# Attention and two MoE layers in one kernel: the sums of s over the later positions taken by one scan for both heads, and later in the lead-in

## Chip, cores and metric

The kernel runs on one core of one Trainium2 chip. The metric is the device time of one execution in microseconds (us); the number quoted for a kernel is the median of its runs.

## What is computed

Three layers follow one another. Attention, for 4 batches and 8 heads of 576 positions and 64 columns, has a bias from running sums of s:

```python
s_pos = np.maximum(s, 0.0)
cum = np.cumsum(s_pos, axis=-1)
bias = -(cum[:, :, :, None] - cum[:, :, None, :])
scores = np.where(causal, -1000000000.0, scores + np.minimum(bias, 0.0))
```

Then softmax over the keys and a product with v. The 2304 x 512 result goes through a first layer, `max(max(x @ w1, x @ w2), x @ w3) @ w_out` with 768 hidden columns, and a second, `((x @ w_a) * (x @ w_b)) @ w_out` with 1536. The change concerns `cum` alone.

## The kernel before

Two heads make a pair; a batch has four pairs, all four 16. A pair is done in two parts: R = 0 is its first 256 positions (`Q0`), R = 1 the other 320 (`N1`). The order of parts is batch by batch, R = 0 of its four pairs, then R = 1. The first layer's products (the gates, `g`, L803) follow each part's output X, with w1, w2, w3 split into a high and a low half (`hg`, `lg`), three products for each block of 128 rows: high by high, low of X by high, high by low. Gate weights come as 18 loads of 512 KB (`wraw`, L244), named w0 to w17 in their order here. Each is made into numbers by ACT (L255) and DVE (L258, L259), rounded by POOL into `hg` (L88), and subtracted by DVE into `lg` (L92). w0, w1, w2 and all from w5 on share three raw buffers, which `lg` frees.

**The lead-in** (`lead_in`, L1051) does R = 0 of the first batch, four pairs p = 0 to 3, before anything else. At the start DVE runs a scan over s of the first 256 positions of both heads (L179): row r of `cum`, on partition 64 + r, holds head 0 in columns 0 to 255 and head 1 in columns 256 to 511, and `reset` puts the sum back to zero between them. The result, multiplied by columns of the identity, becomes extra rows of k and q, so that scores and bias come out of one product. Then for each pair and head: score products on PE (`fs`, L1096), maxima on DVE (L598, one instruction of 128 and one of 256 columns, each with a read of its accumulator), exp and sums on ACT (L605), sum and reciprocal on DVE (L614, L615), the division on POOL (L619, two instructions a head), transposes on PE (`ts`, L710) with copies to SBUF by ACT or DVE (L713), products with v (`pv`, L737), and the split of X into `Xh` (ACT, L81) and `Xl` (DVE, L92). The probabilities have four buffers (tag P), so that pair 2 writes where pair 0 stood, and pair 3 where pair 1 stood.

The sums of the later 320 positions are needed first by R = 1 of this batch. `scan_tails` (L184) makes them after the second pair's maxima: one max with zero over 16 rows x 640 columns (L185), then a scan for each head over 16 x 320 (L188), that begins from the head's sum at position 255, in the same 16 partitions. `store_sums` (L194) writes all sums to DRAM (`ck` for keys, `cq` for queries) by five DMAs on SP's queue; `load_pair` (L494) reads a row of each back into the k and q tiles of a pair, and the first product of R = 1, `fj` (L671), reads those tiles. `store_tails` (L202) later splits the sums in a high and a low half (L204, L205) and stores these (`kt`, `qt`).

What order the instructions of an engine have is settled by a scheduler when the kernel is built, out of priorities (`tc.high_priority`) and its own estimate of each instruction; `issue_after` and, for PE, `on_pe` (L1044) add order by hand. A small edit can therefore change the order for a long way behind it.

Of the kernel before, what the change touches and what calls it, by code (L numbers as in the profile page):

```python
# [29 lines left out]
def kernel(  # L30
# [44 lines left out]
    def f(ap):  # L75
        return ap.bitcast(F32)
# [67 lines left out]
    def pt_tile(shape, dt, nm):  # L144
        return ap_.tile(shape, dt, tag="PT", bufs=2, name=nm)

    def parts(t):

        return (
            t[:, : 2 * Q0].rearrange("r (h c) -> r h c", h=2),  # L150
            t[:, 2 * Q0 : 2 * S].rearrange("r (h c) -> r h c", h=2),
        )

    def spin(n):

        ps = ps_m.tile([P, 512], F32, tag="m", name="spin")
# [11 lines left out]

    cum, sraw = early("KB1"), early("KB2")
    reset, ones = early("QA1")[:, : 2 * Q0], early("QA2")[:, : 2 * Q0]  # L170
    up, rr = slice(64, P), slice(64, 64 + SR)
    with tc.high_priority(5100):
        for a, e in enumerate((nc.sync, nc.scalar, nc.sync, nc.scalar)):
            e.dma_start(sraw[64 + a * SR : 64 + (a + 1) * SR, : 2 * Q0], s[:, : 2 * Q0])
        nc.vector.memset(reset[up], 1.0)
        nc.vector.memset(reset[up, Q0 : Q0 + 1], 0.0)
        nc.vector.memset(ones[up], 1.0)
        nc.vector.tensor_scalar_max(sraw[up, : 2 * Q0], sraw[up, : 2 * Q0], 0.0)
        nc.vector.tensor_tensor_scan(  # L179
            cum[up, : 2 * Q0], reset[up], sraw[up, : 2 * Q0], 0.0,  # L180
            op0=ALU.mult, op1=ALU.add,
        )

    def scan_tails():  # L184
        nc.vector.tensor_scalar_max(sraw[rr, 2 * Q0 :], sraw[rr, 2 * Q0 :], 0.0)  # L185
        for h in range(2):
            c = slice(2 * Q0 + h * N1, 2 * Q0 + (h + 1) * N1)
            nc.vector.tensor_tensor_scan(  # L188
                cum[rr, c], ones[rr, :N1], sraw[rr, c],
                cum[rr, (h + 1) * Q0 - 1 : (h + 1) * Q0],  # L190
                op0=ALU.mult, op1=ALU.add,
            )

    def store_sums(dk, dq, t):  # L194
        a, b = parts(t[rr])
        nc.sync.dma_start(dk[:, :, :Q0], a)
        nc.sync.dma_start(dk[:, :, Q0:], b)
        nc.sync.dma_start(dq[:, 0], b[:, 0])
        nc.sync.dma_start(dq[:, 1, 0:64], b[:, 1, 256:])
        nc.sync.dma_start(dq[:, 1, 64:], b[:, 1, :256])  # L200

    def store_tails():  # L202
        hi = early("KB2", F32R)
        nc.scalar.copy(hi[rr], cum[rr])  # L204
        nc.vector.tensor_tensor(cum[rr], cum[rr], f(hi[rr]), op=ALU.subtract)  # L205
        store_sums(kt[:, 0], qt[:, 0], f(hi))
        store_sums(kt[:, 1], qt[:, 1], cum)

# [367 lines left out]
    def small(nm, w=1):  # L576
        return ap_.tile([P, w], F32, tag="small", bufs=10, name=nm)
# [473 lines left out]
    def lead_in():  # L1051
# [21 lines left out]
                    qq[p][lo_], cum[lo_, : 2 * Q0], AF.Copy, scale=-float(D) ** 0.5  # L1073
                )
        with tc.high_priority(4800):
            nc.sync.dma_start(sraw[rr, 2 * Q0 :], s[0:SR, 2 * Q0 :])
            for p in LP:
                nc.sync.dma_start(lead[p][2], qv0[0, p][:, 2 * Q0 :])
            for j in range(NL):
                fetch_w1(w1_keys[j])  # L1080
# [7 lines left out]
        def fs(p):  # L1088
            for h in range(2):
                pool, tag = (ps_m, "m") if h else (ps_s, "s")  # L1090
                ps = pool.tile([P, 512], F32, tag=tag, name="f0")
                pt = ap_.tile([P, S], F32, tag="P", bufs=4, name="F0")
                for i in range(2):
                    o = ps[:, P * i : P * (2 * i + 1)]
                    def mm(o=o, i=i):
                        last_pe[:] = [nc.tensor.matmul(  # L1096
                            o, two(qq[p])[:, h, i * P : i * P + P],
                            two(kk[p])[:, h, 0 : P * (i + 1)], start=True, stop=True,
                        ).ins]
                    on_pe(mm)  # L1100
                pend.append(sm_a([[(ps[:, 0:P], 0)], [(ps[:, P : 3 * P], P)]], pt, SCALE))
                if len(pend) > 1:
                    with tc.issue_after(pend[-1][-1]):
                        sm_b(pend.pop(0))
                pts[p, h] = pt

        def ts(p):
            if p % 2 == 0:
                shared["PT"] = pt_tile([P, 2, 4 * N1], F32, "PF")
            PF[p] = shared["PT"][:, :, p % 2 * 2 * N1 :]  # L1110
            for h in range(2):
                def tr(h=h):
                    f_t0(PF[p], h, pts[p, h], True)
                on_pe(tr)
# [16 lines left out]

        with tc.high_priority(4000):
            fs(0)
            fs(1)
            with tc.issue_after(pend[-1][-1]):
                scan_tails()
            store_sums(ck, cq, cum)
            fs(2)
            ts(0)
            fs(3)  # L1140
            sm_b(pend.pop(0))
            ts(1)
            pv(0)
            fetch(NP)
            ts(2)
            pv(1)
            fetch(NP + 1)
            ts(3)
            wn()
            pv(2)  # L1150
            wn()
            sp(1)
            pv(3)
            wn(NL - 2)
# [731 lines left out]
```

## Time and profile before

| what | us |
|---|---|
| median of 3 runs (lowest to highest) | 885.6 (884.72 to 887.51) |
| the profiled execution | 884.49 |
| its span, first to last instruction | 882.4 |
| PE busy with matmuls | 869.9 (99%) |
| DVE busy | 632.6 (72%) |
| ACT busy | 394.3 (45%) |
| POOL busy | 210.0 (24%) |

The profile is one execution; 2.1 us of its own time lie outside of the span. Times in the rows further down are us from the start of the span. Engines are PE (matmul; PEld is its weight load), DVE, ACT, POOL, and SP, which issues most DMAs ("SPq"). A matmul's busy time holds its latency, so that neighbours overlap, and two products of one row each cost what their starts are apart. The share of busy time is an average over the span; the lead-in and the stretch behind it differ from it.

### The profile page before, as it was taken

How to read it: one execution, taken by the hardware profiler on the slowest of the kernel's cores; microseconds unless marked ns; L12 is line 12 of the kernel's file. 1: busy time of each engine (PE TensorE's matmuls, PEld its weight loads, DVE VectorE, ACT ScalarE, POOL GpSimd, SP SyncE). 2: the span in 40 equal slices, each digit the busy share in tenths (PEclk: the TensorE clock that was granted, in tenths of full speed). 3: DMA queues.
4: the chain of work that ended last, by engine and by line, in shares of the span. 5: the costliest groups of instructions: out<-in, count | busy, mean ns of one | idle time of the engine just before them, and what ended most of it. 6: DMA issues, size and time to landing. Idle time of an engine off the chain costs nothing.

```text
span 882.4 us, 16782 instructions
## 1 busy us (share of the span) xinstructions
PE 869.9 (99%) x6024; PEld 828.8 (94%) x6024; DVE 632.6 (72%) x1437; ACT 394.3 (45%) x859; POOL 210.0 (24%) x327
## 2 busy tenths in 40 slices
PE   8999999999999999999999999999999999999998
PEld 6767899899999999999999999999999999999998
DVE  7986646575778566664797866777776859987874
ACT  7564745575656545544563323222222224433321
POOL 5445322233423323200003111111111310322211
PEclk9999999999999999999999999999999999999999
DMA  7665634265234853483302134444442353353231
GB/s 231 190 202 175 173 108 130 88 179 149 65 97 116 269 158 122 136 288 122 140 1 72 37 120 137 162 141 159 141 158 93 111 182 123 99 174 129 96 120 49
DMA packets 68219, 120.04 MB, mean 136 GB/s; under 512 B 6920, under 2 KB 50600, under 8 KB 68136
## 3 DMA queue, kind: packets, MB, share of 16 engines
q1 hardware_dynamic: 60944, 111.58, 39.5%
q10 hardware_dynamic: 7192, 7.38, 2.5%
q8 instruction: 48, 0.79, 0.4%
q14 instruction: 35, 0.29, 0.1%
HBM read 87.92 MB, written 31.01 MB: 135 GB/s over the span
## 4 chain that ended last, share of the span: by engine, by line
PE 93%; DVE 3%; DMA 1%; ACT 1%; issue 1%; POOL 1%; ACTq 0%; POOLq 0%; DVEq 0%; SPq 0%
PE X L1252 29%; PE g L803 24%; PE Z L1252 15%; PE Y L1252 8%; PE fpv L737 5%; PE t L755 3%; PE s L627 2%; PE s L628 2%; PE f L671 1%; PE ft L710 1%; DMA wraw<-in_moe_w_dram 1%; PE W L1252 1%; PE tj L768 1%; PE sj L662 1%; PE sj L661 1%
## 5 line engine op out<-in xcount | busy, mean ns | idle before, releaser
L803 PE MATMUL g<-Xh,hg 128*128 128x320 f32 (+1 forms) x576 | 175.1, 307 | 0.6 <-POOL hg L88 0.5
L803 PE MATMUL g<-Xh,lg 128*128 128x256 f32 (+1 forms) x576 | 173.5, 302 | 1.2 <-DVE lg L92 1.2
L803 PE MATMUL g<-Xl,hg 128*128 128x256 f32 (+1 forms) x576 | 172.3, 300 | 0.0
L803 PEld LDWEIGHTS g<-Xh,hg 128*128 128x128 f32 x576 | 108.4, 189 | 5.9 <-issue 2.5
L803 PEld LDWEIGHTS g<-Xh,lg 128*128 128x128 f32 x576 | 108.7, 189 | 3.7 <-DVE lg L92 2.7
L803 PEld LDWEIGHTS g<-Xl,hg 128*128 128x128 f32 x576 | 108.8, 189 | 1.8 <-issue 0.7
L88 POOL TENSOR_SCALAR wh<-wval 128x256 fp32r<-128x256 f32 x77 | 40.9, 540 | 275.5 <-DVE wval L343 226.5
L1252 PE MATMUL X<-xh,wh 128*128 128x384 f32 x288 | 97.2, 338 | 0.0
L1252 PE MATMUL X<-xl,wh 128*128 128x384 f32 x288 | 96.9, 336 | 0.0
L1252 PE MATMUL X<-xh,wl 128*128 128x384 f32 x288 | 96.9, 337 | 0.0
L1252 PE MATMUL X<-woh,slot 128*128 128x256 f32 x408 | 76.6, 281 | 0.5 <-ACT ob L1299 0.5
L619 POOL TENSOR_SCALAR P<-P,rs 128x128 f32<-128x128 f32 (+2 forms) x80 | 48.1, 607 | 101.5 <-DVE rs L615 71.7
L356 DVE TENSOR_TENSOR slot<-hraw,slot 128x768 fp32r<-128x768 f32 x60 | 60.3, 1031 | 13.8 <-POOL slot L88 11.1
L356 DVE TENSOR_TENSOR u<-Z,u 128x384 f32<-128x384 f32 x72 | 39.6, 551 | 37.9 <-ACT u L1299 28.2
L1252 PEld LDWEIGHTS X<-woh,slot 128*128 128x128 f32 x408 | 64.3, 189 | 0.7 <-ACT ob L1299 0.7
L812 DVE TENSOR_TENSOR hf<-g,hf 128x256 f32<-128x256 f32 (+1 forms) x96 | 43.5, 453 | 27.6 <-PE g L803 19.5
L605 ACT ACTIVATE P<-P,nm 128x128 f32<-128x128 f32 (+2 forms) x80 | 46.7, 584 | 35.8 <-DVE nm L598 24.6
L1252 PE MATMUL X<-wol,slot 128*128 128x256 f32 x204 | 57.0, 280 | 0.0
L81 ACT ACTIVATE slot<-hraw 128x768 fp32r<-128x768 f32 x39 | 32.5, 846 | 51.3 <-DVE hraw L356 24.3
L1252 PEld LDWEIGHTS X<-xh,wh 128*128 128x128 f32 x288 | 54.1, 188 | 0.5 <-DVE u L356 0.3
L1252 PEld LDWEIGHTS X<-xl,wh 128*128 128x128 f32 x288 | 54.1, 188 | 0.0
L1252 PEld LDWEIGHTS X<-xh,wl 128*128 128x128 f32 x288 | 54.1, 188 | 0.0
(211 smaller groups left out, 2210.2 us busy)
## 6 DMA issues: line engine op xcount, KB each, us to landing
hT<-u SPq DMA_DIRECT2D x72, 192.0 KB
hraw<-hT SPq DMA_DIRECT2D x36, 384.0 KB
wraw<-in_moe_w_dram SPq DMA_DIRECT2D x18, 512.0 KB
wraw<-in_moe_w_out_dram SPq DMA_DIRECT2D x18, 512.0 KB
kraw<-in_kT_dram SPq DMA_DIRECT2D x24, 288.0 KB
wraw<-in_moe_w_a_dram SPq DMA_DIRECT2D x12, 512.0 KB
wraw<-in_moe_w_b_dram SPq DMA_DIRECT2D x12, 512.0 KB
st<-h1T SPq DMA_DIRECT2D x24, 192.0 KB
```

The source lines that it names most:

```text
L81: return nc.scalar.activation(o, i, AF.Copy, scale=scale)
L88: nc.gpsimd.tensor_scalar(o, i, scale, 1.0, op0=ALU.mult, op1=ALU.mult)
L356: return {"V": nc.vector, "P": nc.gpsimd}[e].tensor_tensor(o, a, b, op=op)
L605: e_ = nc.scalar.activation(pt[:, c0:c1], pt[:, c0:c1], AF.Exp, bias=first, scale=-1.0, accum_out=sm[:, g : g + 1],)
L619: n_ = nc.gpsimd.tensor_scalar(pt[:, c0:c1], pt[:, c0:c1], rs[:, g : g + 1], 1.0, op0=ALU.mult, op1=ALU.mult,)
L627: nc.tensor.matmul(ps, QA1[:, qs], KB1[:, h, ksl], start=True, stop=False)
L628: nc.tensor.matmul(ps, QA2[:, qs], KB2[:, h, ksl], start=False, stop=True)
L737: e_ = nc.tensor.matmul(ps[h * D : h * D + D, c0:n], w, x, start=(t == 0), stop=(t == len(mm[h]) - 1),)
L755: nc.tensor.transpose(ps[:, j * P : j * P + P], pt[:, j * P : j * P + P], ident)
L803: nc.tensor.matmul(ps[:, :n], w[:, kk, :], x[:, kk, :], start=(i == 0), stop=(i == len(mm) - 1),)
L812: st["V"] = nc.vector.tensor_tensor(hf, ps[:, :n], hf, op=ALU.max)
L1252: e_ = nc.tensor.matmul(ps[:, :n], w, x, start=(first and i == 0), stop=(i == len(mm) - 1), skip_group_check=not first,)
```

## The change

The sums of the later positions move to partitions 0 to 63: head 0 of the 16 rows on partitions 0 to 15, head 1 on 32 to 47, both in columns 0 to 319, so that one scan of 64 partitions does both heads. Its initial values, the sums at position 255, lie on other partitions (64 + r): two products on PE with rows of the identity bring them into a PSUM tile (`find_off`), and ACT copies them to SBUF. The rows that no load fills are set to zero by a memset, `ones` is filled on all partitions, and the load of the later s becomes two DMAs. `scan_tails` and `store_sums` are called after the maxima of the last pair instead of the second. Stores of 320 columns that were one DMA for both heads are now two, six DMAs in place of five; `store_tails` makes its split in two pieces (16 x 512 and 64 x 320).

```diff
--- before.py
+++ after.py
@@ -144,13 +144,6 @@
     def pt_tile(shape, dt, nm):
         return ap_.tile(shape, dt, tag="PT", bufs=2, name=nm)
 
-    def parts(t):
-
-        return (
-            t[:, : 2 * Q0].rearrange("r (h c) -> r h c", h=2),
-            t[:, 2 * Q0 : 2 * S].rearrange("r (h c) -> r h c", h=2),
-        )
-
     def spin(n):
 
         ps = ps_m.tile([P, 512], F32, tag="m", name="spin")
@@ -168,41 +161,64 @@
 
     cum, sraw = early("KB1"), early("KB2")
     reset, ones = early("QA1")[:, : 2 * Q0], early("QA2")[:, : 2 * Q0]
-    up, rr = slice(64, P), slice(64, 64 + SR)
+    up, rr, tl = slice(64, P), slice(64, 64 + SR), slice(0, 64)
+    w0 = slice(0, 2 * Q0)
     with tc.high_priority(5100):
         for a, e in enumerate((nc.sync, nc.scalar, nc.sync, nc.scalar)):
-            e.dma_start(sraw[64 + a * SR : 64 + (a + 1) * SR, : 2 * Q0], s[:, : 2 * Q0])
+            e.dma_start(sraw[64 + a * SR : 64 + (a + 1) * SR, w0], s[:, w0])
         nc.vector.memset(reset[up], 1.0)
         nc.vector.memset(reset[up, Q0 : Q0 + 1], 0.0)
-        nc.vector.memset(ones[up], 1.0)
-        nc.vector.tensor_scalar_max(sraw[up, : 2 * Q0], sraw[up, : 2 * Q0], 0.0)
+        nc.vector.memset(ones, 1.0)
+        nc.vector.memset(sraw[tl, :N1], 0.0)
+        nc.vector.tensor_scalar_max(sraw[up, w0], sraw[up, w0], 0.0)
         nc.vector.tensor_tensor_scan(
-            cum[up, : 2 * Q0], reset[up], sraw[up, : 2 * Q0], 0.0,
-            op0=ALU.mult, op1=ALU.add,
+            cum[up, w0], reset[up], sraw[up, w0], 0.0, op0=ALU.mult, op1=ALU.add
         )
 
+    def load_tails():
+        for h in range(2):
+            nc.sync.dma_start(
+                sraw[32 * h : 32 * h + SR, :N1],
+                s[:, 2 * Q0 + h * N1 : 2 * Q0 + (h + 1) * N1],
+            )
+
+    off = []
+
+    def find_off():
+
+        off.append(ps_m.tile([P, 512], F32, tag="m", name="off"))
+        for h in range(2):
+            last_pe[:] = [nc.tensor.matmul(
+                off[0][32 * h : 32 * h + 32, :1], ident[up, 64:96],
+                cum[up, (h + 1) * Q0 - 1 : (h + 1) * Q0], start=True, stop=True,
+            ).ins]
+        o = small("off")
+        nc.scalar.copy(o[tl], off[0][tl, :1])
+        off[0] = o
+
     def scan_tails():
-        nc.vector.tensor_scalar_max(sraw[rr, 2 * Q0 :], sraw[rr, 2 * Q0 :], 0.0)
-        for h in range(2):
-            c = slice(2 * Q0 + h * N1, 2 * Q0 + (h + 1) * N1)
-            nc.vector.tensor_tensor_scan(
-                cum[rr, c], ones[rr, :N1], sraw[rr, c],
-                cum[rr, (h + 1) * Q0 - 1 : (h + 1) * Q0],
-                op0=ALU.mult, op1=ALU.add,
-            )
+        t = sraw[tl, :N1]
+        nc.vector.tensor_scalar_max(t, t, 0.0)
+        nc.vector.tensor_tensor_scan(
+            cum[tl, :N1], ones[tl, :N1], t, off[0][tl], op0=ALU.mult, op1=ALU.add
+        )
 
     def store_sums(dk, dq, t):
-        a, b = parts(t[rr])
-        nc.sync.dma_start(dk[:, :, :Q0], a)
-        nc.sync.dma_start(dk[:, :, Q0:], b)
-        nc.sync.dma_start(dq[:, 0], b[:, 0])
-        nc.sync.dma_start(dq[:, 1, 0:64], b[:, 1, 256:])
-        nc.sync.dma_start(dq[:, 1, 64:], b[:, 1, :256])
+        b = [t[32 * h : 32 * h + SR, :N1] for h in range(2)]
+        nc.sync.dma_start(
+            dk[:, :, :Q0], t[rr, w0].rearrange("r (h c) -> r h c", h=2)
+        )
+        nc.sync.dma_start(dk[:, 0, Q0:], b[0])
+        nc.sync.dma_start(dk[:, 1, Q0:], b[1])
+        nc.sync.dma_start(dq[:, 0], b[0])
+        nc.sync.dma_start(dq[:, 1, 0:64], b[1][:, 256:])
+        nc.sync.dma_start(dq[:, 1, 64:], b[1][:, :256])
 
     def store_tails():
         hi = early("KB2", F32R)
-        nc.scalar.copy(hi[rr], cum[rr])
-        nc.vector.tensor_tensor(cum[rr], cum[rr], f(hi[rr]), op=ALU.subtract)
+        for r, c in ((rr, w0), (tl, slice(0, N1))):
+            nc.scalar.copy(hi[r, c], cum[r, c])
+            nc.vector.tensor_tensor(cum[r, c], cum[r, c], f(hi[r, c]), op=ALU.subtract)
         store_sums(kt[:, 0], qt[:, 0], f(hi))
         store_sums(kt[:, 1], qt[:, 1], cum)
 
@@ -1073,7 +1089,7 @@
                     qq[p][lo_], cum[lo_, : 2 * Q0], AF.Copy, scale=-float(D) ** 0.5
                 )
         with tc.high_priority(4800):
-            nc.sync.dma_start(sraw[rr, 2 * Q0 :], s[0:SR, 2 * Q0 :])
+            load_tails()
             for p in LP:
                 nc.sync.dma_start(lead[p][2], qv0[0, p][:, 2 * Q0 :])
             for j in range(NL):
@@ -1131,13 +1147,14 @@
 
         with tc.high_priority(4000):
             fs(0)
+            on_pe(find_off)
             fs(1)
+            fs(2)
+            ts(0)
+            fs(3)
             with tc.issue_after(pend[-1][-1]):
                 scan_tails()
             store_sums(ck, cq, cum)
-            fs(2)
-            ts(0)
-            fs(3)
             sm_b(pend.pop(0))
             ts(1)
             pv(0)
```

The scheduler orders the program anew: PE's order differs from its first products up to about its 890th row, then it is the same as before. Lines of the changed kernel are 16 or 17 higher from L200 on (its L614 is the maxima, L598 before; its L630 and L631 are sum and reciprocal, its L819 the gates, L687 `fj`). Numbers in names are the scheduler's and differ between the two.

On DVE, in the lead-in, before, from the end of the second pair's maxima (`F_261`) to the third's second head (`F_301`); `eKB` is `cum` or the raw s, `ft` are transposes:

```order
L598 ISA F_261,nm<-f_260,maskJ 128x256
L598 ISA nm 128x1
L185 TENSOR_SCALAR eKB_116<-eKB_116 16x640
L614 TENSOR_SCALAR rs<-sm 128x2
L598 ISA F_285,nm<-f_284,maskJ 128x128
L598 ISA nm 128x1
L188 SCALAR_TENSOR_TENSOR eKB_115<-eQA_118,eKB_115,eKB_116 16x320
L615 RECIPROCAL rs<-rs 128x2
L188 SCALAR_TENSOR_TENSOR eKB_115<-eQA_118,eKB_115,eKB_116 16x320
L598 ISA F_285,nm<-f_284,maskJ 128x256
```

and in the changed kernel, from the last pair's maxima (`F_343`, second head) on:

```order
L729 COPY PF<-ft_375 128x384
L614 ISA F_343,nm<-f_342,maskJ 128x256
L614 ISA nm 128x1
L201 TENSOR_SCALAR eKB_116<-eKB_116 64x320
L630 TENSOR_SCALAR rs<-sm 128x2
L202 SCALAR_TENSOR_TENSOR eKB_115<-eQA_118,off,eKB_116 64x320
L631 RECIPROCAL rs<-rs 128x2
L92 TENSOR_TENSOR Xl<-fpv,Xh 128x256
L729 COPY PF<-ft_404 128x384
L630 TENSOR_SCALAR rs<-sm 128x2
L631 RECIPROCAL rs<-rs 128x2
```

The max and the scan now stand behind the last maxima, ahead of the last pair's two reciprocals (L631).

On PE, at the end of the lead-in, before, from the last product with v:

```order
L737 MATMUL fpv<-PF,kqv 64x256 x2
L737 MATMUL fpv<-PF,kqv 64x128 x2
L671 MATMUL fj<-kraw,qvraw 64x288 x4
L803 MATMUL g<-Xh,hg_0_140 128x256
L803 MATMUL g<-Xl,hg_0_140 128x256
L803 MATMUL g<-Xh,lg_0_141 128x256
```

and in the changed kernel, from the end of the first gate (12 products, here its last two) on:

```order
L819 MATMUL g<-Xl,hg_0_141 128x256
L819 MATMUL g<-Xh,lg_0_142 128x256
L687 MATMUL fj<-kraw,qvraw 64x288 x4
L819 MATMUL g<-Xh,hg_0_143 128x256
L819 MATMUL g<-Xl,hg_0_143 128x256
L819 MATMUL g<-Xh,hg_0_145 128x256
L819 MATMUL g<-Xl,hg_0_145 128x256
L819 MATMUL g<-Xh,hg_1_147 128x256
L819 MATMUL g<-Xl,hg_1_147 128x256
L687 MATMUL f_500<-kraw,qvraw 128x384
```

`fj`, the first product of R = 1, stood ahead of all gates and stands now behind the first gate; behind it come the first two products of each of the next three gates, ahead of the next scores (`f_500`).

On DVE again, some 20 us later, before: the low half of w7 (`lg_2_155`) and of w8 (`lg_2_157`), and the first step of w9 (L258):

```order
L615 RECIPROCAL rs<-rs 128x1
L258 TENSOR_SCALAR wraw<-wraw 128x512
L92 TENSOR_TENSOR lg_2_155<-wraw,hg_2_154 128x512
L598 ISA FJ,nm<-fj,maskJ,nm 128x288
L598 ISA nm 128x1
L92 TENSOR_TENSOR lg_2_157<-wraw,hg_2_156 128x512
```

and in the changed kernel (`lg_2_156` is w7's, `lg_2_158` w8's, L274 the step on w9):

```order
L631 RECIPROCAL rs<-rs 128x1
L92 TENSOR_TENSOR lg_2_156<-wraw,hg_2_155 128x512
L614 ISA FJ,nm<-fj,maskJ,nm 128x288
L614 ISA nm 128x1
L274 TENSOR_SCALAR wraw<-wraw 128x512
L92 TENSOR_TENSOR lg_2_158<-wraw,hg_2_157 128x512
```

w9's first step stood ahead of w7's low half and stands now behind it, still ahead of w8's.

On SP, the first `kt` and `qt` stores of `store_tails` stand now ahead of the loads of the third pair's R = 1 rows, where they stood behind them.

## Rows read from the trace of the kernel before

**Rows 1.** Page, part 1: busy time, share of the span, instructions.
```profile
PE 869.9 (99%) x6024; PEld 828.8 (94%) x6024; DVE 632.6 (72%) x1437; ACT 394.3 (45%) x859; POOL 210.0 (24%) x327
```
**Rows 2.** Waits of PE, 24 to 70 us, the longest: for whom, total, times, longest.
```profile
PE g L803 <- DVE lg L92: 1.2, 2, 0.9
PE t L755 <- POOL F L619: 0.5, 1, 0.5
PE g L803 <- POOL hg L88: 0.5, 1, 0.5
```
**Rows 3.** Waits of PE, 70 us to the end; longest row.
```profile
PE s L628 <- POOL P L619: 1.3, 1, 1.3
```
**Rows 4.** Timeline, the later sums on DVE: start, duration, engine, line, what.
```profile
10.78 0.52 DVE L185 TENSOR_SCALAR eKB<-eKB 16x640 f32<-16x640 f32 x1
...
11.89 0.88 DVE L188 TENSOR_TENSOR_SCAN eKB<-eQA,eKB,eKB 16x320 f32<-16x320 f32 x1
...
12.99 0.87 DVE L188 TENSOR_TENSOR_SCAN eKB<-eQA,eKB,eKB 16x320 f32<-16x320 f32 x1
```
**Rows 5.** Timeline, lead-in: other engines and the last pair's maxima.
```profile
11.51 0.19 ACT L605 ACTIVATION_READ_ACCUMULATOR F<-F,nm 128x1 f32 x1
...
11.97 1.48 PE L1096 MATMUL f<-kqv 128*128 128x128 f32 x8
...
14.64 0.55 DVE L713 COPY PF<-ft 128x384 f32<-128x384 f32 x1
...
17.99 0.41 DVE L598 CUSTOM_DVE_ANT_0 F<-f,maskJ 128x256 f32<-128x256 f32 x1
...
20.12 0.82 POOL L619 TENSOR_SCALAR F<-F,rs 128x128 f32<-128x128 f32 x2 [0.42 <-DVE rs L615]
```
**Rows 6.** Timeline, DVE at the start and at the split of the sums.
```profile
3.41 0.56 DVE L178 TENSOR_SCALAR eKB<-eKB 64x512 f32<-64x512 f32 x1 [0.49 <-DMA eKB<-in_s_dram]
...
55.52 1.73 DVE L205 TENSOR_TENSOR eKB<-eKB,eKB 16x1152 f32<-16x1152 f32 x1
```
**Rows 7.** Timeline, PE from the lead-in's end: `fj`, first gate, first later scores.
```profile
23.84 1.17 PE L671 MATMUL fj<-kraw,qvraw 66*64 66x288 f32 x8
...
24.94 0.39 PE L803 MATMUL g<-Xh,hg 128*128 128x256 f32 x1
...
27.09 0.91 PE L671 MATMUL f<-kraw,qvraw 66*128 66x384 f32 x2 [0.21 <-DVE nm L598]
```
**Rows 8.** Chain that ended last: twelve gate products in a row.
```profile
76.84 1.43 PE g L803 x12
```
**Rows 9.** Timeline, steps of a gate weight, apart and beside each other.
```profile
21.91 0.69 DVE L259 SCALAR_TENSOR_TENSOR wraw<-wraw 128x512 int32<-128x512 int32 x1
...
22.69 0.64 POOL L88 TENSOR_SCALAR hg<-wraw 128x512 fp32r<-128x512 f32 x1 [1.74 <-DVE wraw L259]
...
28.16 1.73 DVE L259 SCALAR_TENSOR_TENSOR wraw<-wraw 128x512 int32<-128x512 int32 x2
...
29.37 2.09 POOL L88 TENSOR_SCALAR hg<-wraw 128x512 fp32r<-128x512 f32 x2 [0.63 <-DVE wraw L259]
```
**Rows 10.** Timeline, SP: stores of the later sums, reads of their rows.
```profile
13.90 0.60 SPq L197 DMA_DIRECT2D ck<-eKB  x1
...
19.14 0.27 SPq L492 DMA_DIRECT2D kraw<-ck  x1
...
20.08 0.22 SPq L492 DMA_DIRECT2D qvraw<-cq  x1
```
**Rows 11.** Timeline, DVE at 45 us: w9's first step, w7's low half.
```profile
45.03 0.43 DVE L258 TENSOR_SCALAR wraw<-wraw 128x512 int32<-128x512 int32 x1 [1.62 <-DMA wraw<-in_moe_w_dram]
...
45.38 0.68 DVE L92 TENSOR_TENSOR lg<-wraw,hg 128x512 fp32r<-128x512 f32 x1
```
**Rows 12.** Busy by stretch: PE, PEld, DVE, ACT, POOL, then granted clock, DMA share, GB/s.
```profile
13.90:17.35 3.45, 2.14 (x14) 1.16 (x14) 2.81 (x18) 2.73 (x11) 2.50 (x7) 1.00 1.04 374
17.35:20.76 3.41, 3.41 (x19) 2.04 (x16) 2.42 (x11) 1.88 (x7) 2.01 (x6) 0.50 0.29 74
```

## The prediction

> **What bounds the kernel now.** I read the busy times first, then the waits of PE, then the timeline of the lead-in. PE is busy for 99% of the span [rows 1]. Its waits from 24 to 70 us are 2.2 us in the three longest rows [rows 2], and of those behind 70 us the longest sum is 1.3 us [rows 3], so from the first gates on PE's own work is nearly the bound, and a change that adds no more to PE than two tiny products can win only what PE loses before that: the lead-in, up to the first gate product at 24.94 [rows 7], and those 2.2 us. All of it together is a small part of 884 us. What lies in the lead-in: DVE does the later sums for 0.52 + 0.88 + 0.87 = 2.27 us between 10.78 and 13.86 [rows 4], with two maxima of the third pair on either side of them. The last pair's last maxima end at 17.99 + 0.41 = 18.40, the last division on POOL at 20.12 + 0.82 = 20.94 [rows 5], and 4.0 us later the gates begin.
>
> **The lead-in, step by step.** Taken out of DVE: 2.27 us ahead of the last maxima [rows 4]. Not all of it comes off, since two other things wait. The last pair's maxima write the buffers from which the second pair is transposed, and those transposes stand on PE behind the last score products, which end at 11.97 + 1.48 = 13.45 [rows 5], unmoved; with three transposes behind them, 0.5, the first of the last maxima can start at 14.0. From there DVE's queue to the last maxima is two heads of 128 and 256 columns (0.41 for the larger, some 0.3 for the smaller), a copy of 0.55 [rows 5], and five sums and reciprocals that run into one another, 1.9 us in all: it ends at 15.9, 2.5 us sooner.
> Put in behind it: a max over 320 columns, between nothing and the 0.52 that 640 columns took [rows 4], taken as 0.35 from 0.56 for 512 [rows 6]; and one scan over 64 x 320. No row has that shape; 16 x 320 took 0.88, and twice that bounds it above. I take 0.88, since the time of DVE's rows goes with columns. The scan ends at 17.2 and the two reciprocals of the last pair come behind it. Between them stand a split of X over 256 columns (0.4, as the maxima of that width) and a copy of 0.55 [rows 5]; with 0.5 for the small ones and POOL's start the last division begins at 18.65 and ends, 0.82 later, at 19.45: 1.5 us sooner than 20.94.
> From the last division to the gates before: 4.0 us, in which `fj` takes 24.94 - 23.84 = 1.1 [rows 7]. `fj` now follows the first gate, so 2.9 remain: gates from 22.35, twelve products in 1.43 [rows 8], done at 23.8. Before, `fj` and that gate were done near 26.4.
>
> **The small edits together.** A zero memset of 320 columns on DVE is shorter than the 0.49 us for which DVE waited for s [rows 6]: nothing, and were that cover gone 0.3. ACT's copy of 64 x 1 stands in the first exps; its nearest row is 0.19 [rows 5], and it moves the second pair's sums by 0.2, which the 14.0 above already hides; between nothing and 0.2. The two products of one column on PE stand where PE waits for maxima anyway; 0 to 0.3 (two of twelve in [rows 8]). One more load of s on SP stands ahead of the gate weights, whose second step runs first at 21.91 [rows 9]: nothing, up to 0.6, one issue as in [rows 10]. The split of the sums on DVE takes 832 columns for 1152: 1.73 x 832 / 1152 = 1.25 [rows 6], 0.5 less, there where PE waited 0.5 for a division [rows 2]; I count 0.2. The `kt` and `qt` stores now block SP in front of the third pair's rows until the split is made; this costs nothing, as the `fj` of that pair stands 28 products further back in PE's new order, some 3 us by [rows 8].
>
> **Behind the lead-in the gain is mostly spent.** After the first gate PE wants weights. The last product with v ends where the gates begin, at 22.35; 0.85 later, for `Xh` and `Xl`, at 23.2, DVE has the last split of X behind it, then three steps L258 (0.43 each, [rows 11]) to 24.4, then four L259 in a row while POOL rounds. Alone a step takes 0.69 and a rounding 0.64; beside each other two took 1.73 and two 2.09 [rows 9], so 0.87 and 1.05. First L259 to 25.1, roundings to 26.0, 27.05 and 28.1. PE's order has products of all three weights ahead of the next scores: these start at 28.1 + 0.24 = 28.35, with 18 gate products done. Before, they started at 27.09 with 14 done [rows 7]. Four products are 0.48, so at this place the new kernel is 1.26 - 0.48 = 0.8 **behind**. The low halves are then all made early, and before the change PE still had waits ahead of it: 0.3 of the 1.2 and the 0.5 of [rows 2], and latency with them, 1.0. Balance at 32 us: 0.2 ahead, and 1.2 if the steps run at their lone times. I take 0.4, near the first, as the four now overlap as those rows did.
> Here a page speaks against the change. The Trainium skill, SBUF — State Buffer, section "Who interferes with whom", says that a DVE instruction with two SBUF inputs and a GpSimd instruction that reads SBUF exclude each other for the whole instruction. Its result is a rival below.
> At 45 us DVE waited 1.62 for w9 and w7's low half stood behind that [rows 11]; PE lost 0.9 there [rows 2]. Now w7's half is ahead of it. w8's is still behind, but PE needs it some 20 products (2.4 us) later, so the 0.9 goes, unless w9 is later: I count 0.7.
>
> **Sum**, against the profiled execution's 884.49: 0.4 + 0.7 + 0.2 = 1.3 sooner, 883.2. The median shown is 885.6, 1.1 above that execution, so the median forecast is **884.3**. A measurement of this kernel can tell about 0.3%, 2.7 us, from no change.
>
> **`fj` and its rows.** The scan ends at 17.2, and five stores follow on SP, at 0.6 each, as the issue of 13.90 took [rows 10]: the last at 19.8. Before, the key row was asked for 19.14 - 13.90 = 5.24 after its store was issued, and `fj` ran 23.84 - 20.08 = 3.76 after the last row was asked for [rows 10, 7]. Both are upper bounds, 28.8 together; below, only the issues count, 20.4. `fj` may start as late as 28.1 - 1.17 - 0.5 = 26.4 without moving anything. I take it as in time: before, the store lay behind weights at a DMA share of 1.04, and the share from 17.35 on was 0.29 [rows 12].
> The Trainium skill, DMA: Bandwidth & Descriptors, section "Anatomy of one DMA — SWDGE (gpsimd) path", gives a fixed cost of some 2 us for a transfer on another kind of queue; by it, an estimate, `fj` would start near 24.1, and the sum would stay. No run here shows a transfer alone.
>
> **Rivals.**
> *The lead is kept whole*: conversions at lone times and no wait in their place. 2.6 of the lead-in and 0.9 at 45 us, 3.5 in all: 882.1. For it: POOL stood idle for 1.74 ahead of its first rounding [rows 9]. Against it: the four steps in a row. 0.13.
> *Slower, through `fj`*: it stands ahead of three gates, and its rows leave SP some 4 us later. At the upper bound it runs from 28.8, the next scores start at 28.8 + 1.17 + 0.7 = 30.7 for 28.35, and 1.3 sooner becomes 1.0 later: 886.6. It decides from 26.4 on. For it: PE has nothing else in order. Against it: the empty DMA queues. 0.12.
> *The clock*: from 17.35 to 20.76 PE ran at 0.50 (1.2 of 2.4 GHz), after a stretch with 2.14 us busy of 3.45, waiting for divisions [rows 12]. If that fall comes instead while gates run, as long a stretch costs at most 1.7, less the waits in it, 1.2: 885.5. 0.10.
> *Nothing gained*: DVE and POOL shut each other out in the gate steps. Four times 0.69 and three times 0.64, one behind the other from 24.4, end the third rounding at 29.1, 1.0 later: 0.3 sooner in all, 885.3. For it: in the rows of two [rows 9] a step took a quarter longer than alone and a rounding two thirds; against it: they ran side by side all the same. This is what the Trainium skill's page SBUF — State Buffer would make of it. 0.12.
> The forecast has 0.53.
>
> **How the numbers follow.** Range: the lower end takes in the first rival and half a microsecond of scatter (the runs shown lie 0.9 below to 1.9 above their median), 881.6; the upper the `fj` rival, 887.0. Faster by over 0.3% (under 882.9): most of the first rival and the edge of the forecast, 0.16. Slower (over 888.3): `fj` or the clock together with scatter, 0.07. Between: 0.77.
>
> **What would show it.** Right: last maxima near 15.9, one scan of 0.9 behind them, first gate near 22.3, PE idle between `fj` and 28 us for `hg`, no wait at 45 us. Wrong: a scan well over 1 us; `fj` late with a wait on the rows' DMAs; a half clock behind 21 us; or PE short of weights w13 to w17 because SP stood before the `kt` stores, of which I have counted nothing.

## The result, and the profile after

| | median | ratio to before, 95% interval | profiled execution: span |
|---|---|---|---|
| before | 885.17 us (6 runs here) | 1 | 882.4 us |
| the change | 889.83 us (889.31 to 892.52, 6 runs) | 1.0061 [1.0050, 1.0072] | 887.3 us |

Slower by 4.7 us, where 884.3 was forecast and the range ended at 887.0. PE's part of the page answers to [rows 1]: it works 3 us longer for two products (four matrix instructions) more, a sign that it ran more slowly.

```profile
PE 873.1 (98%) x6028; PEld 830.5 (94%) x6028; DVE 634.2 (71%) x1438; ACT 395.7 (45%) x861; POOL 214.5 (24%) x327
```

Next the waits of PE from 24 to 70 us, which answer to [rows 2]: low halves cost 0.2 where they cost 1.2, but hg 2.0 for 0.5, and one division alone 1.9.

```profile
PE g L819 <- POOL hg L88: 2.0, 3, 0.9
PE t L771 <- POOL F L635: 1.9, 1, 1.9
PE g L819 <- DVE lg L92: 0.2, 1, 0.2
```

Behind 70 us little changed: the longest wait is 1.4 for 1.3 [rows 3], though it is now one for a DMA (`vraw`), and the two behind it are 0.5 and 0.2 in both. So the loss lies ahead of 75 us. The busy shares of that stretch, first before, then the change (columns as in [rows 12]):

```profile
13.90:75.00 61.10, 56.91 (x374) 41.55 (x375) 52.77 (x159) 36.38 (x89) 30.38 (x45) 0.97 0.62 197
```
```profile
13.90:75.00 61.10, 54.66 (x341) 39.32 (x342) 49.88 (x138) 32.27 (x79) 27.87 (x36) 0.92 0.58 180
```

PE is idle for 6.44 us instead of 4.19, and the mean clock is 0.92 instead of 0.97. From 13.9 to 75 us, in windows cut at its changes, the clock is at 0.50 three times, where before it was so once [rows 12]. The first, third and fifth row below are at the lower level (1.2 of 2.4 GHz); the second and fourth are what PE did ahead of the later two falls.

```profile
20.62:24.04 3.42, 3.42 (x16) 1.96 (x18) 1.92 (x4) 0.95 (x2) 0.47 (x1) 0.50 0.48 137
26.07:30.86 4.79, 2.79 (x16) 1.61 (x16) 4.79 (x10) 0.89 (x3) 3.76 (x4) 1.00 0.54 171
30.87:34.28 3.41, 3.41 (x15) 3.00 (x14) 2.79 (x6) 0.87 (x2) 0.39 (x1) 0.50 0.60 187
61.00:64.99 3.99, 1.99 (x17) 1.58 (x15) 3.38 (x11) 1.18 (x3) 3.81 (x3) 1.00 0.85 213
65.00:68.41 3.41, 3.41 (x18) 2.70 (x18) 1.07 (x1) 0.96 (x2) 0.67 (x2) 0.50 0.98 351
```

Ahead of both PE was busy for about half the time, and DVE and POOL for most of it. The account: 2.25 us more idle, and 6.83 us more at half speed, worth 3.4 at most; 5.7 together as an upper bound, for a span that is 4.9 longer.

**The lead-in.** DVE and POOL, answering to [rows 4, 5]:

```profile
15.80 0.41 DVE L614 CUSTOM_DVE_ANT_0 F<-f,maskJ 128x256 f32<-128x256 f32 x1
...
16.14 0.31 DVE L201 TENSOR_SCALAR eKB<-eKB 64x320 f32<-64x320 f32 x1
...
16.49 0.88 DVE L202 TENSOR_TENSOR_SCAN eKB<-eQA,off,eKB 64x320 f32<-64x320 f32 x1
...
19.43 0.69 DVE L275 SCALAR_TENSOR_TENSOR wraw<-wraw 128x512 int32<-128x512 int32 x1
```
```profile
18.83 1.64 POOL L635 TENSOR_SCALAR F<-F,rs 128x128 f32<-128x128 f32 x2 [0.39 <-DVE rs L631]
19.46 1.01 POOL L635 TENSOR_SCALAR F<-F,rs 128x256 f32<-128x256 f32 x1
```

The last maxima end at 16.2 (18.40 before), the scan takes 0.88 over 64 rows as over 16. But the last division takes 1.64 where it took 0.82 [rows 5]. It is two instructions (the second row is its second one alone): the first, 0.64, stands beside the step L274 of the first weight (18.90 to 19.32), the second, 1.01, beside L275. PE's last products with v then meet the half clock, and the first gate comes at 24.44, 0.5 sooner than in [rows 7].

**24 to 31 us.** DVE, POOL, PE:

```profile
26.32 3.38 DVE L275 SCALAR_TENSOR_TENSOR wraw<-wraw 128x512 int32<-128x512 int32 x4
```
```profile
27.10 4.16 POOL L88 TENSOR_SCALAR hg<-wraw 128x512 fp32r<-128x512 f32 x4 [6.01 <-DVE wraw L275]
```
```profile
26.07 1.19 PE L687 MATMUL fj<-kraw,qvraw 66*64 66x288 f32 x8
28.17 0.39 PE L819 MATMUL g<-Xh,hg 128*128 128x256 f32 x1 [0.91 <-POOL hg L88]
29.21 0.39 PE L819 MATMUL g<-Xh,hg 128*128 128x256 f32 x1 [0.54 <-POOL hg L88]
30.26 0.39 PE L819 MATMUL g<-Xh,hg 128*128 128x256 f32 x1 [0.55 <-POOL hg L88]
```

Four steps at 0.69 and four roundings at 0.64 would be 2.76 and 2.56 alone; they take 3.38 and 4.16, and PE gets a weight every 1.05 us.

**62 to 65 us.** A 128x512 division on POOL (0.7 us where it stands alone) beside two DVE instructions that read two tensors in SBUF:

```profile
62.07 2.41 POOL L635 TENSOR_SCALAR F<-F,rs 128x512 f32<-128x512 f32 x1
```
```profile
62.64 0.67 DVE L92 TENSOR_TENSOR lg<-wraw,hg 128x512 fp32r<-128x512 f32 x1
63.24 0.68 DVE L275 SCALAR_TENSOR_TENSOR wraw<-wraw 128x512 int32<-128x512 int32 x1
```
```profile
64.54 0.73 PE L771 MATMUL t<-ident,F 128*128 128x128 f32 x4 [1.88 <-POOL F L635]
```

L275 ends at 63.92, the division 0.56 later. So the theory (A) that the runs were to test: the edit moves the scheduler's order (between the tables of runs 2 and 4 below, which hold the same instructions, some 280 rows of PE stand elsewhere, all among its first 1,100); in the new order POOL's work stands beside DVE's with two operands, PE goes short, and behind that its clock falls. Rivals: the place alone costs (B), the new form costs with its loads, stores and split (C), the clock falls whatever PE does (D).

### The profile page after: what moved, and what is told of

It is laid out like the page before. It is cut to its first block, busy times and chain, and to the rows that moved or that the text cites. A ratio compares the mean times of both kernels' runs of the same rounds, so it can differ in the third digit from the quotient of the medians.

```text
span 887.3 us, 16796 instructions
## 1 busy us (share of the span) xinstructions
PE 873.1 (98%) x6028; PEld 830.5 (94%) x6028; DVE 634.2 (71%) x1438; ACT 395.7 (45%) x861; POOL 214.5 (24%) x327
## 4 chain that ended last, share of the span: by engine, by line
PE 92%; DMA 3%; DVE 2%; issue 1%; POOL 1%; ACT 1%; SPq 0%; ACTq 0%; POOLq 0%
PE X L1269 29%; PE g L819 24%; PE Z L1269 14%; PE Y L1269 8%; PE fpv L753 5%; PE t L771 3%; PE s L643 2%; PE s L644 2%; PE f L687 2%; DMA wraw<-in_moe_w_dram 1%; PE W L1269 1%; PE ft L726 1%; PE tj L784 1%; PE sj L678 1%; PE sj L677 1%
## 5 line engine op out<-in xcount | busy, mean ns | idle before, releaser
L819 PE MATMUL g<-Xh,hg 128*128 128x320 f32 (+1 forms) x576 | 175.2, 307 | 2.2 <-POOL hg L88 2.0
L819 PE MATMUL g<-Xh,lg 128*128 128x256 f32 (+1 forms) x576 | 174.4, 304 | 0.2 <-DVE lg L92 0.2
L819 PE MATMUL g<-Xl,hg 128*128 128x320 f32 (+1 forms) x576 | 173.4, 302 | 0.0
L819 PEld LDWEIGHTS g<-Xh,hg 128*128 128x128 f32 x576 | 109.4, 191 | 6.6 <-POOL hg L88 3.2
L819 PEld LDWEIGHTS g<-Xh,lg 128*128 128x128 f32 x576 | 109.8, 191 | 1.9 <-DVE lg L92 1.3
L819 PEld LDWEIGHTS g<-Xl,hg 128*128 128x128 f32 x576 | 109.8, 191 | 1.5 <-issue 0.5
L635 POOL TENSOR_SCALAR P<-P,rs 128x128 f32<-128x128 f32 (+2 forms) x80 | 48.8, 614 | 103.5 <-DVE rs L631 69.2
L828 DVE TENSOR_TENSOR hf<-g,hf 128x256 f32<-128x256 f32 (+1 forms) x96 | 43.6, 454 | 25.2 <-PE g L819 19.8
```

Of the source, the lines that this page charges most:

```text
L635: n_ = nc.gpsimd.tensor_scalar(pt[:, c0:c1], pt[:, c0:c1], rs[:, g : g + 1], 1.0, op0=ALU.mult, op1=ALU.mult,)
L819: nc.tensor.matmul(ps[:, :n], w[:, kk, :], x[:, kk, :], start=(i == 0), stop=(i == len(mm) - 1),)
L828: st["V"] = nc.vector.tensor_tensor(hf, ps[:, :n], hf, op=ALU.max)
```

## The experiments

Some runs hold each engine's order: an issue-order edge from every instruction to the one ahead of it on its engine, by a table taken from a built kernel, in which only the rows named are moved. There the line numbers stand 9 higher (L644 is L635; with the added products 11 or more). Ratios are to the kernel before on the same chip. Differences from the change are of medians, taken on different chips; by the ratios each comes out 0.1 to 1.3 us better.

**1. The place alone**: the old maximum and two scans, moved.

```diff
             fs(1)
-            with tc.issue_after(pend[-1][-1]):
-                scan_tails()
-            store_sums(ck, cq, cum)
             fs(2)
             ts(0)
             fs(3)
+            with tc.issue_after(pend[-1][-1]):
+                scan_tails()
+            store_sums(ck, cq, cum)
```

> The kernel before with one thing moved: its old maximum and two old scans (16 rows, both heads one after the other) stand behind the last pair's maxima. No new load, product, copy, scan or split. The engines' orders differ from the kernel before in some 20 rows of PE and 60 of DVE, all in the lead-in. Theory A (the loss of the change comes from the reshuffled order behind the lead-in: DVE and POOL shut each other out, PE goes short, and its clock falls a second and a third time): no second fall of the clock, 884 to 886 us. Rival B (the place: maxima that end sooner start the gates into unready weights, in whatever order): 888 us or more. Rival C (the new form costs: added loads, stores, split): as theory A here, since the form is not in.

887.09 us, 1.0028 [1.0017, 1.0038]: between the theories. The order behind the lead-in is that of before and PE's waits there are nearly so (low halves 0.8 for 1.2); what is new lies in the lead-in, where PE waited for divisions for 1.5 us in all before (same view), and where the half clock now lasts 6.83 us instead of 3.41:

```profile
PE ft L710 <- POOL F L619: 3.4, 4, 1.4
```
```profile
20.67:27.50 6.83, 5.95 (x26) 3.70 (x27) 3.43 (x7) 1.60 (x4) 2.53 (x4) 0.50 0.57 153
```

None of the twelve runs has a mean clock above 0.996, where 29 of the 30 of before beside them have 0.997 or more. How much of the loss is the waits and how much the clock, the run does not tell.

The place is no gain: the two scans still stand ahead of the reciprocals for the last divisions, and now nothing else is left for DVE to do beside them. In the old form rival B thus holds for 2.6 us.

**2. The whole change in that order.**

```diff
+    for row in ORDER:
+        row = [held[int(x)] for x in row.split()]
+        for a, z in zip(row, row[1:]):
+            tc.add_manual_dep(z, a.name, NoSync)
```

> The whole change, every new instruction in it, but each engine's instructions held in the order of the run with the place alone (the order of before behind the lead-in; the added instructions stand where their old counterparts stood). Theory A (the order): one fall of the clock only, 884 to 886 us, 3.5 us or more faster than the change as it is. Rival B (the place): 888 or more. Rival C (the form): 888 or more, with PE waiting for rows or weights behind the stores.

884.77 us, 0.9996 [0.9985, 1.0007]: as theory A, by the medians 5.1 us faster than the same instructions in the scheduler's own order. C is out, and of B little is left with the shorter scan. The first gate comes 3 us sooner than in [rows 7], with no half clock between 13.9 and 75 us:

```profile
21.92 0.36 PE L828 MATMUL g<-Xh,hg 128*128 128x256 f32 x1
```
```profile
13.90:75.00 61.10, 57.57 (x391) 42.57 (x392) 54.48 (x155) 37.12 (x90) 33.69 (x46) 1.00 0.66 207
```

That is one execution. Each run lists its mean clock, in which one stretch of 3.41 us at half speed makes 3.41 / 2 / 885 = 0.002. At 0.999 or above the four runs of this kernel average 882.84, the eleven of before beside it 884.19: 1.35 less. That this is near the forecast's sum of 1.3 is luck, since the sum was made for the scheduler's own order, with other gates and waits. The other eight runs, at 0.996 to 0.998, average 885.3, so that the median of all shows no gain.

**3. PE kept busy where it idled**, order held.

```diff
+            w, x, kk = mm[0]
+            for _ in range({(0, 0, 0, 1): 5, (0, 0, 0, 2): 5, (0, 0, 4, 0): 14}.get((b, R, m, g), 0)):
+                nc.tensor.matmul(ps[:, :n], w[:, kk, :], x[:, kk, :], start=True, stop=True)
...
+                for _ in range(3 if first_fj else 0):
+                    nc.tensor.matmul(o[:, :HS], qn[0:66, h, 256:320], kn[0:66, h, 0:HS], start=True, stop=True)
```

> The change, each engine's order held as it is, and 27 products more on PE where it stood idle: 3 repeats of fj's first product ahead of fj, 5 repeats each of the first product of the second and third gate, 14 of the first product of a gate at 62.2 us. Each repeat writes what the product behind it writes again. If it is the idle time ahead of them that makes the clock fall (theory A): no half clock at 30.9 to 34.3 and at 65.0 to 68.4; each of these two costs up to 1.7 us now, so 886.4 to 888 us. Rival D (the falls come at these places whatever PE does): half clock at both places, 889.5 to 891 us.

888.82 us, 1.0040 [1.0026, 1.0054]: both falls are gone in the profile, but the gain is 1.0 (1.9 by the ratios) instead of 1.8 to 3.4. The two stretches at full clock:

```profile
30.87:34.28 3.41, 3.41 (x28) 3.14 (x27) 3.21 (x9) 0.87 (x2) 0.56 (x1) 1.00 0.57 173
65.00:68.41 3.41, 3.41 (x27) 2.64 (x27) 0.99 (x4) 1.54 (x4) 0.30 (x1) 1.00 0.92 255
```

28 matrix instructions run there for 15 in the change, 27 for 18. In the first stretch two are score products in both kernels and the rest gate products (of the 28, five are added ones); thirteen at 0.12 (1.43 / 12, [rows 8]) are 1.55 us, an estimate of the price of one stretch that falls on gates. Where the rest went: in this execution the first fall lasted 6.83 us instead of 3.41, from 19.9 on, ahead of every edit (in run 4's too, from 19.5), and near 300 us a wait for a DMA is 2.3 for 1.4. The two of the seven runs with a mean clock of 0.998 average 886.8, 3.1 less than the change; the other five, at 0.996, 889.0. So it was the idle time that made the clock fall at these two places (D is out there), but how long the fall in the lead-in lasts differs between executions of the same instructions.

**4. The division apart from DVE's pair**, order held.

```diff
   L274 wraw            (61.56 us)
   L828 hf<-g,hf
-  L92  lg<-wraw,hg
-  L275 wraw<-wraw
   L630 rs<-sm
   L828 hf<-g,hf
   L631 rs<-rs
+  L92  lg<-wraw,hg
+  L275 wraw<-wraw
```

> The change, each engine's order held, but two instructions of DVE moved: the low half lg (L92) and the weight step L275 that stand at 62.6 and 63.2 us, beside the 128x512 division which took 2.41 there, now stand behind the five small ones that follow them. Theory A (DVE instructions with two operands in SBUF and POOL's shut each other out): the division takes 0.7 to 1.2, PE's transposes start 1.2 to 1.7 us sooner, lg comes 0.5 late at most, and with PE less idle the clock need not fall at 65.0: 886.5 to 888.7 us. Rival E (the division is long for another reason, such as DMA traffic in SBUF): it still takes over 2 us, 889.8 us.

886.97 us, 1.0028 [1.0018, 1.0039]: 2.9 less than the change, near the better end of A's range. (The two were moved behind three instructions, where the expectation says five.) The division takes 0.86, beside L828 (`hf`, on DVE) and the small ones; PE waits 0.33 for it, and the clock stays up there.

```profile
60.97 0.86 POOL L644 TENSOR_SCALAR F<-F,rs 128x512 f32<-128x512 f32 x1
```
```profile
61.89 0.66 PE L780 MATMUL t<-ident,F 128*128 128x128 f32 x4 [0.33 <-POOL F L644]
```

Nothing else was moved, so the 2.41 was DVE's pair (rival E is out).

**5. The first weight's steps behind the copy**, order held.

```diff
   L92  Xl<-fpv,Xh      (18.58 us)
-  L274 wraw
-  L275 wraw<-wraw
   L729 PF<-ft
+  L274 wraw
+  L275 wraw<-wraw
   L92  lg<-wraw,hg
```

> The change, each engine's order held, but the first weight's two steps on DVE (L274 and L275 at 18.9 and 19.4 us) put behind the copy of the last transposes (L729 at 21.2). Theory A (POOL's last division took 1.64 because DVE's steps stood beside it): the last two divisions take 0.8 to 0.9 and end at 19.7, not 20.5; the copy and the last products with v come 0.7 sooner; but the first gate's weight is then made behind the copy, which takes 0.42 + 0.69 + 0.64 = 1.75 from 20.9 on, so gates near 23.5 to 24.4. The time 889 to 890 us, since the lull at 26 to 30 us and the one at 62 stay. Rival F (the forecast's own step: gates end sooner by what the division gains and this lasts to the end): 888.5 us or less.

891.82 us, 1.0069 [1.0043, 1.0095]: a miss by a microsecond or two, on the bad side, and by the intervals not told apart from the change (1.0050 to 1.0072). The step itself does what it should: the division is back at 0.83 and the first gate comes at 23.24 instead of 24.44, still at half clock. But PE then waits for the second weight all the longer, and the clock falls at 30.7, for 6.83 us at 64.9, and once more at 300.4, behind a wait of 1.84 for a DMA.

```profile
18.74 0.83 POOL L644 TENSOR_SCALAR F<-F,rs 128x128 f32<-128x128 f32 x2 [0.39 <-DVE rs L640]
```
```profile
28.25 0.39 PE L828 MATMUL g<-Xh,hg 128*128 128x256 f32 x1 [1.90 <-POOL hg L96]
```

What the lead-in wins is lost at the next thing that is late, as long as the weights are made in that order, and rival F, by which the gain lasts to the end, is out for the median. One of the six runs, the only one at 0.998 (the others have 0.990 to 0.994), took 884.99: a single run, but it points to the clock for most of what this kernel loses.

**6. The steps spread**, order held; DVE first, then PE.

```diff
   L274 wraw (w1)
+  L275 wraw (w1)
   L92  Xl<-fpv,Xh
-  L274 wraw (w2), (w3), (w4)
-  L275 wraw (w1), (w2), (w3), (w4)
-  L614 FJ<-fj
-  L92  lg (w1), (w2), (w3)
-  L614 FJ<-fj
+  L274, L275 wraw (w2); L92 lg (w1); L614 FJ<-fj
+  L274, L275 wraw (w3); L92 lg (w2); L614 FJ<-fj
+  L274, L275 wraw (w4); L92 lg (w3)
   L92  lg (w4)
   fj x4
-  g (w1) x2, g (w2) x2, g (w3) x2, f, g (w1) x10, g (w2) x10
+  g (w1) x12, f, g (w2) x12, g (w3) x2
```

> The change, each engine's order held, but for 24 to 33 us: on DVE the four steps L275 no longer stand in a row; the second weight's comes right behind its L274, where DVE idled 1.1 us, and each other one is followed by a low half or a maximum; on PE the second gate's products stand together and the next scores behind them. Theory A (the row of four beside POOL's four roundings makes PE wait 2.0 us for hg, and the clock falls behind that): no wait for hg over 0.5 there, no half clock at 30.9, 1.5 to 3.7 us less: 886 to 888.3 us. Rival D (the fall comes anyway, and later waits take up what is won): 889 us or more.

886.60 us, 1.0022 [1.0011, 1.0033]: 3.2 less, as A has it. No wait for hg is left, and no fall near 31 us. What stays is the wait at the division, 1.9, and the clock falls right behind it:

```profile
60.40:62.58 2.18, 0.31 (x3) 0.27 (x3) 1.76 (x6) 0.29 (x1) 2.18 (x2) 1.00 0.75 196
62.58:65.99 3.41, 3.41 (x18) 2.94 (x18) 1.07 (x1) 0.96 (x2) 0.87 (x2) 0.50 1.00 364
```

**7. Both** (the moves of 4 and 6 in one table).

> Both reorderings of DVE in one kernel: the steps L275 at 24 to 33 us spread, and the low half and the step at 62 to 64 us put behind the division. Theory A: the gains add, 3.0 us of the second and 1.5 to 3.7 of the first: 883 to 885.5 us, as the change in the old order. Rival (one loss hides the other): no better than the better of the two, 886.5 us.

884.71 us, 0.9996 [0.9987, 1.0006]: the 5.1 us of run 2 again, from two moves on DVE and one on PE. So these two places make up the loss, as far as the intervals tell. Not every wait is gone: the spread steps make PE wait for low halves, in short pieces behind which this profile shows no half clock:

```profile
PE g L828 <- DVE lg L100: 2.2, 5, 0.8
```

**8. The form alone, at the old place**, order left to the scheduler.

```diff
             fs(1)
+            with tc.issue_after(pend[-1][-1]):
+                scan_tails()
+            store_sums(ck, cq, cum)
             fs(2)
             ts(0)
             fs(3)
-            with tc.issue_after(pend[-1][-1]):
-                scan_tails()
-            store_sums(ck, cq, cum)
```

> The new form at the old place: two loads, products on PE, one scan over 64 rows, six stores and the split in two, but the maximum and the scan stand behind the second pair's maxima as before, one scan of 0.88 us shorter. The orders differ from the kernel before in 312 rows of PE. Theory A: what counts is which order results behind the lead-in, so 884 to 887 us with at most one fall of the clock more than before. Rival C (the form costs, in loads, stores and split): 887 us or more with PE waiting for a DMA.

883.40 us, 0.9987 [0.9976, 0.9998]: below what A gave, 1.5 us faster than before, with an interval that just leaves out 1. The sums take 0.46 + 0.97 us where they took 2.27 [rows 4], and the first gate is at 21.79.

```profile
10.63 0.46 DVE L201 TENSOR_SCALAR eKB<-eKB 64x320 f32<-64x320 f32 x1
11.13 0.97 DVE L202 TENSOR_TENSOR_SCAN eKB<-eQA,off,eKB 64x320 f32<-64x320 f32 x1
```

With runs 1 and 2 this makes a square: old form, old place 1; old form, new place 1.0028; new form, old place 0.9987; new form, new place 0.9996 in the order of run 1, and 1.0061 in the scheduler's. The form gains at both places; the place loses 0.3% in the old form, and in the new one less than the intervals can tell; the order decides the rest. The square is not a clean one, since run 8 has an order of its own (312 rows of PE differ from before).

**9. The form alone, and the steps spread**: the table of run 8 with its rows moved much as in 6 (on PE both next score products ahead of the second weight's).

```diff
   L274 wraw (w1)
   L92  Xl<-fpv,Xh
+  L275 wraw (w1)
+  L274 wraw (w2); L614 FJ<-fj; L614 FJ<-fj; L92 lg (w1)
+  L275 wraw (w2); L274 wraw (w3); L92 lg (w2)
...
-  L275 wraw (w1); L614 FJ<-fj
-  L275 wraw (w2), (w3), (w4)
```

> The new form at the old place, each engine's order held, but with the weight steps L275 at 23 to 28 us spread among low halves and maxima and the second gate's products together, as in the run with the steps spread. That kernel's PE waited 0.86 and 0.55 us for hg there. Theory A: both waits go and nothing takes their place at once: 0.7 to 1.4 us less than the form at the old place, 882.0 to 882.7 us, the fastest of all. Rival (the waits return as waits for low halves or later): 883 to 884 us.

881.63 us, 0.9969 [0.9957, 0.9980]: 3.0 us faster than before. All six runs have a mean clock of 1.000. Its steps alone, spread in the old form, were not run, so how the 3.0 divides between form and spread is open. PE's waits from 13.9 to 75 us, to be held against 6.0 us of the change and 4.3 of before in the same view:

```profile
PE ft L735 <- POOL F L644: 0.9, 3, 0.5
PE g L828 <- DVE lg L100: 0.6, 1, 0.6
PE f L696 <- DVE nm L623: 0.3, 1, 0.3
```

**10. Run 7 with PE busy in the lead-in**: 14 products of the identity in three idle stretches.

```diff
             pv(1)
+            spin(14)
             fetch(NP + 1)
```

> The change with both reorderings of DVE (steps spread, division apart), and 14 products of the identity with itself more on PE in the lead-in, 5, 4 and 5 of them in the three idle stretches of 0.6 us each at 17.4 to 20.5, ahead of the transposes that wait for POOL's divisions. If it is this idle time that makes the clock fall near 20 us (theory A): runs at a mean clock of 0.998 and above become the rule, and the median falls from 884.7 to 883 to 884 us. Rival D (the fall near 20 us comes from something else than PE's idle time in the lead-in): clocks as without the added products, 884.5 to 885.3 us.

885.95 us, 1.0016 [1.0004, 1.0029]: a miss. The clocks rose as expected (nine of eleven runs at 0.998 or above, four of eleven in run 7), but the time did not fall with it: the eight runs at 0.998 average 886.3, the six of run 7 at 0.996 884.8, so the mean clock alone does not explain these times. Each added product is two matrix instructions, so they took more than the idle time and the first gate is 0.4 later than in run 7 (23.04 for 22.64). And in the profile the fall comes elsewhere, from 292.7 to 299.5 us, behind a wait of PE for a DMA of 2.83, where run 7 has one of 1.5:

```profile
293.84 0.55 PE L653 MATMUL s<-KB,QA 128*128 128x256 f32 x1 [2.83 <-DMA QA<-kt]
```

A fall in the lead-in lies partly on waits; one there lies on products alone. In the other profiles the wait at that place is 1.0 to 2.3, and the clock fell behind it in run 5's alone (1.84). Why that DMA was late is open, and with it where the rest of the time went.

## Why the prediction was wrong, by its own steps

Against the profiled execution the sum was 0.4 for the lead-in and the stretch behind it, 0.7 at 45 us and 0.2 for the split. The 0.7 held in size. The 0.4 failed: the gates began 2.1 later than forecast, and PE waited 2.0 for `hg`. The 0.2 became a loss, with 1.9 of wait. And a term was missing, two more stretches at half clock, 3.4 us at most. Of the signs of being wrong that the prediction named, one came: a half clock behind 21 us.

- **Last maxima at 15.9, scan 0.88, max 0.35.** Right: 16.2, 0.88 and 0.31.
- **"The last division begins at 18.65 and ends, 0.82 later, at 19.45."** The first step that failed. It began at 18.83 and took 1.64. The forecast moved the division forward at its old length, without the weight's steps that DVE does beside it in the new order; run 5 moves these away and measures 0.83.
- **"So 2.9 remain: gates from 22.35."** Wrong by 2.1: one from the division, and the other from the half clock, which now lies on the products with v and the transposes (20.62 to 24.04) instead of the waits ahead of them. In run 7's profile, with the division as slow but the clock up, the first gate is at 22.64.
- **The four steps in a row.** The rate was right: 3.7 us forecast from the first step to the third rounding, 3.9 measured (26.32 to about 30.2, where the third rounding ends; its gate starts at 30.26). All of it came 2 us later, since the gates did, so "0.2 ahead" at 32 us became a lull with 2.0 us of waits.
- **"The clock", rival at 0.10.** The mechanism was right, the count was not: it priced one stretch that falls on gates, at 1.2 to 1.7, and asked only where the old one would go. Two more came behind the lulls, by run 3 some 1.55 for one of them. This is the missing term of the sum.
- **The split of the sums: "0.5 less; I count 0.2".** The wrong sign. The two splits take 2.10 together for 1.73; in runs 2 and 8, with a division of POOL beside them but no rounding, they take 1.58, so the count of columns left out what POOL does beside them. And the new order put a low half and a step beside the division behind them: 1.9 us of wait for 0.5 [rows 2], and a half clock behind that. Run 4 gives 2.9 back.
- **"Nothing gained", rival at 0.12.** Its mechanism is the one at work: DVE and POOL shut each other out. The Trainium skill, SBUF — State Buffer, section "Who interferes with whom", says so of DVE instructions with two SBUF inputs and GpSimd's that read SBUF; the traces agree (the division 2.41 beside such a pair, 0.86 without). The prediction applied it to the gate steps alone and not to POOL's divisions, and priced it without the clock that goes with the waits.
- **`fj`, rival at 0.12.** Not so: it ran at 26.07 without a wait, when 26.4 was the limit.
- **45 us.** Right in size: the 0.9 went, the low halves cost 0.2. That it was the new order's doing is not shown: in run 2, with the old one, they cost 0.3, and DVE waits 0.49 for w9 there instead of 1.62.
- **Loads, stores, copy, two products at nothing.** Right within what the intervals tell, by runs 2 and 8.

## What to carry to other kernels

An edit in a scheduled kernel is two edits, its instructions and the order that results: hold the old order by edges and time the new instructions in it, before either is judged. When work moves forward, list what will then stand beside it on DVE and POOL, for where DVE reads two tensors in SBUF the overlap was paid for here by one or both, and the price of a wait on PE can be the wait plus a slower clock behind it. Here what was worth keeping was the form; with the weight steps spread out the two gave 0.3%, and the place by itself lost.

## What I had not expected of the hardware

- The clock fell after a lull in which no single wait was longer than 0.91 us and PE was busy for 2.79 of 4.79 us (26.07 to 30.86). A stretch lasted 3.41 or 6.83 us, and the same instructions met one or the other, or none, in different executions: 33 of 75 runs of the kernel before have a mean clock of 0.999 or above, none of the change has more than 0.996.
- A DVE step with one tensor waits for POOL too: L274, 0.43 us [rows 11], took 0.83 from 61.56 and ended 0.29 after the rounding beside it (61.18 and 0.92). L828, one of whose two inputs is in PSUM, kept its length beside the division (0.41 both times).
